# Head, seams and tail of a linear-attention-plus-MLP kernel: transposed weights from two queues, a root on another engine, work units placed anew

## The chip, the cores and the metric

The kernel runs on one core of a Trainium2 chip. The metric is the device time of one execution in microseconds (us). The core has five engines that work side by side, each through its own queue of instructions in order: PE (TensorE, matrix products; its weight loads are listed as PEld), DVE (VectorE), ACT (ScalarE), POOL (GpSimd) and SP (SyncE, which here only starts transfers). Transfers are started from the queues of SP and ACT and carried out by 16 DMA engines.

## The reference

Two branches share one input. `x` has 2048 rows of 512 numbers in bf16. Branch A is a linear attention of 32 heads of 16 with a learned feature map (softmax of a projection and of its negative); branch B is a two-layer network with the Mish activation and 1792 hidden units. Cut to what matters:

```python
xn = layernorm(x)                                   # eps 1e-5, no scale
q, k, v = heads(xn @ wqkv)                          # 32 heads of 16
pq, pk = q @ w_phi[h], k @ w_phi[h]
phi_q = concat(softmax(pq), softmax(-pq))           # 32 features
phi_k = concat(softmax(pk), softmax(-pk))
kv = sum_s phi_k[s]^T v[s];  z = sum_s phi_k[s]
o = (phi_q @ kv) / (phi_q @ z + 1e-6)
act = mish(xn @ w1 + b1)
out = x + o @ wo + act @ w2
```

## The kernel before

**Tiling.** The 2048 rows are 16 tiles of 128 rows, in four groups of four (`NT`, `NG`, `TPG`). The contraction over 512 is cut into four blocks of 128 (`KT`), the 1792 hidden units into 14 blocks (`FT`). The program is written in the order in which each engine issues it (a manual schedule), and a tile framework adds the waits between engines that the data and the buffers ask for. A queue never reorders: an instruction that waits holds up everything behind it on its engine.

**Weights.** `w_phi` is folded into the key and query weights. `load_turned` (L87) fetches 512 columns of `wqkv` transposed, with a DMA transpose, into `wT`; `fold` (L93) multiplies its four blocks with the block-diagonal `Wbd` (16 products of 128x128 in all) and evicts four results, to `wkp` for the keys at the start and to `wqp` for the queries in stage 2. In `fold` at the start ACT evicts three blocks and DVE one.

**Normalisation.** `ln_stats` (L110) takes the statistics of tiles on DVE and computes one over the root on POOL, as a power of -0.5 in two instructions; `ln_apply` (L125) writes the normalised tile `xn` on DVE. The first four tiles are then turned on PE (`ln_turn_pe`, four transposing products into PSUM and a copy into `xnT`), the others by DMA transposes of two tiles each (`ln_turn_dma`).

**Units of work on PE.** `project` (L149) makes 4 products of 128x128 by 128x512 into one PSUM buffer; `value` (L159) evicts it into `vext`, `logits` (L186) into `p_sb`. `hidden(n)` (L168) does the next n of the 56 first-layer units (4 groups times 14 blocks, group by group), each 4 products and one Mish on ACT into `acts`. `accumulate(g)` (32 small products into `pkv`) adds up keys times values for one group. `second_layer(t)` makes 14 products into `po`, `attend(h, i)` 8 small ones into `pnd`, whose four copies run on ACT, `project_out(h)` four for each of two tiles on top of `po`; `residual` adds x on DVE and stores. PSUM has five buffers for everything tagged `mm`, and one for `pkv` and `pnd`.

**Units of work on DVE and ACT.** `extremes(s)` subtracts maxima and minima of 16 on DVE; `exponentials(s)` is two instructions of 2048 on ACT; `normalise` sums and divides on DVE. For the queries `turn` then transposes the features by DMA into `qT`. `combine(h)` makes the denominators and weights on DVE for two tiles, adds the two halves and transposes the result by one DMA into `oT`.

**The order.** At the head: loads, constants, 12 warm-up products on an identity, statistics of tiles 0 to 3, `fold`, the four turns among the first logits, then `extremes(0)` with the normalisation of group 1 in its midst, four values, four hidden units. Then a loop over stages s = 0 to 3, written out as

```python
exponentials(s); accumulate(s - 1); value x2 (dve); logits(s + 1) x4 (act); value x2 (act)
ln_stats; normalise(s, 0) with ln_apply of group s + 2 inside; normalise(s, 1)
hidden((16, 14, 8, 10, 4)[s]); extremes(s + 1)
```

(stages 4 and 5 are the queries of groups 0 and 1). After it come `exponentials(4)`, `accumulate(3)`, `mask_kv`, `logits(5)`, `second_layer(0)`, `hidden(4)`, `extremes(5)`, `attend(0, 0)`, `second_layer(1)`, `attend(0, 1)`, `combine(0)`, `exponentials(5)`, and then a loop over eight pairs of tiles, h = 0 to 7, that interleaves `combine`, `project_out`, the logits of the last two query groups, `attend` for two pairs ahead and `second_layer` for two pairs ahead.

**The start of the queues.** SP: x tiles 0 and 1, `wT`, x tiles 4 to 7, `wv`, `w1`, x tiles 8 to 15. ACT: `wsrc` (w_phi), x tiles 2 and 3, `b1b`, then its first table load. Scalar activations need a table; each change between copies, Exp and Mish shows as a table load of 1.28 us.

Of the kernel before, what the change touches and what calls it, by code (L numbers as in the profile page):

```python
# [8 lines left out]
BF16 = mybir.dt.bfloat16  # L9
FP32 = mybir.dt.float32  # L10
# [7 lines left out]
def kernel(  # L18
# [12 lines left out]
    nc = tc.nc  # L31
# [52 lines left out]

    def load_turned(base_col):  # L87

        wT = lnp.tile([P, 4, 512], BF16, name="wT", tag="xn")
        nc.sync.dma_start_transpose(out=wT[:], in_=A_wqkv[:, base_col : base_col + D])  # L90
        return wT

    def fold(wT, dst, dve):  # L93

        for kt in range(KT):
            pf = ps.tile([P, 512], FP32, name="pfold", tag="mm")
            for j in range(4):
                nc.tensor.matmul(
                    pf[:, j * P : (j + 1) * P],
                    lhsT=wT[:, j, kt * P : (kt + 1) * P],  # L100
                    rhs=Wbd[:, j, :],
                    start=True,
                    stop=True,
                )
            if kt in dve:
                nc.vector.tensor_copy(dst[:, kt, :], pf[:])
            else:
                nc.scalar.copy(dst[:, kt, :], pf[:])
# [16 lines left out]
    def ln_apply(t0, n, mv, rstd, xn, at):  # L125
        for i in range(n):
            nc.vector.tensor_scalar(
                out=xn[:, at + i, :],
                in0=x_sb[:, t0 + i, :],
                scalar1=mv[:, i, 0:1],  # L130
                scalar2=rstd[:, i : i + 1],
                op0=ALU.subtract,
                op1=ALU.mult,
            )
# [172 lines left out]
            in1=KVmask[:, 128:136], op0=ALU.add, op1=ALU.mult,  # L307
        )

    nd_of, oT_of, po_of = {}, {}, {}  # L310

    def attend(h, i):

# [24 lines left out]
        )  # L338
        nc.scalar.copy(ds[:, i, :, :, 3, :], b.rearrange("p l (x h) -> p l x h", x=2))  # L339

    def combine(h):

        nm, ds = nd_of.pop(h)
        ds = ds[:].rearrange("p i l x j h -> p i l x (j h)")
        u = opool.tile([P, 2, 2, 32], FP32, name="u")
        w = opool.tile([P, 2, 32], FP32, name="w")
        f = opool.tile([P, 2, 2, 32, 2], BF16, name="f")
        ob = lnp.tile([P, 4, 512], BF16, name="ob", tag="xn")
        o_t = ob[:, 0:2, :]
        oT_of[h] = ob[:, 2:4, :].rearrange("p i (j c) -> p (i j) c", c=P)  # L350
        nc.vector.tensor_tensor(  # L351
            out=u[:], in0=ds[:, :, :, 0, :], in1=ds[:, :, ::-1, 1, :], op=ALU.mult
        )
        nc.vector.tensor_tensor(out=w[:], in0=u[:, :, 0, :], in1=u[:, :, 1, :], op=ALU.add)
        nc.vector.reciprocal(w[:], w[:])  # L355
        nc.vector.tensor_tensor(
            out=u[:], in0=ds[:, :, ::-1, 1, :],
            in1=w[:, :, None, :].to_broadcast([P, 2, 2, 32]), op=ALU.mult,
        )
        nc.vector.tensor_copy(  # L360
            f[:].rearrange("p i l c o -> p (i l c) o"),
            u[:].rearrange("p i l (c o) -> p (i l c) o", o=1).to_broadcast([P, 128, 2]),
        )
        v = nm.rearrange("p i l (c e o) -> p (i l c) e o", e=8, o=2)
        nc.vector.tensor_tensor(  # L365
            out=v, in0=v,
            in1=f[:].rearrange("p i l c o -> p (i l c) o")[:, :, None, :].to_broadcast([P, 128, 8, 2]),
            op=ALU.mult,
        )
        nc.vector.tensor_tensor(  # L370
            out=o_t, in0=nm[:, :, 0, :], in1=nm[:, :, 1, :], op=ALU.add
        )
        nc.sync.dma_start_transpose(out=oT_of[h], in_=o_t.rearrange("p i c -> p (i c)"))

    def second_layer(t):
        po = ps.tile([P, 512], FP32, name="po", tag="mm")
        po_of[t] = po
        for f in range(FT):
            nc.tensor.matmul(  # L379
                po[:], lhsT=acts[:, f, t * P : (t + 1) * P], rhs=w2_sb[:, f, :],  # L380
                start=(f == 0), stop=False,
            )

    def project_out(h):
        for i in range(2):
            po = po_of.pop(2 * h + i)
            for j in range(4):
                nc.tensor.matmul(  # L388
                    po[:], lhsT=oT_of[h][:, i * 4 + j, :], rhs=wo_sb[:, j, :],
                    start=False, stop=(j == 3),  # L390
                )
            residual(2 * h + i, po)

    def residual(t, po):
        y = x_sb[:, t, :]
        nc.vector.tensor_tensor(out=y, in0=po[:], in1=y, op=ALU.add)  # L396
        nc.sync.dma_start(o_v[:, t, :], y)


    nc.sync.dma_start(x_sb[:, 0:2, :], x_v[:, 0:2, :])  # L400
    with nc.allow_non_contiguous_dma(reason="tiny w_phi load"):
        nc.scalar.dma_start(wsrc[:], wphi_v)
    wT = load_turned(D)
    nc.scalar.dma_start(x_sb[:, 2:4, :], x_v[:, 2:4, :])
    nc.scalar.dma_start(b1b[:], b1_v[:, :])
    nc.sync.dma_start(x_sb[:, 4:8, :], x_v[:, 4:8, :])
    nc.sync.dma_start(wv[:], wqkv_v[:, :, 2 * D : 3 * D])
    nc.sync.dma_start(w1_sb[:], w1_v[:, :, :])
    nc.sync.dma_start(x_sb[:, 8:16, :], x_v[:, 8:16, :])

# [14 lines left out]
    nc.vector.tensor_copy(KVmask[:, 0:P], block[:].rearrange("p h d -> p (h d)"))  # L425
    nc.vector.tensor_copy(KVmask[:, P : P + 8], block[:, :, 0])
    nc.vector.tensor_copy(
        kvm[:].rearrange("p l j c -> p (l j) c")[:, :, 136:144],
        block[:, None, :, 0].to_broadcast([P, 8, 8]),
    )  # L430
# [2 lines left out]
    dve, act = nc.vector.tensor_copy, nc.scalar.copy  # L433

    warm = ps.tile([P, 4, P], FP32, name="warm", tag="mm")
    for _ in range(12):
        nc.tensor.matmul(
            warm[:], lhsT=ident[:], rhs=ident[:, None, :].to_broadcast([P, 4, P]),
            start=True, stop=True,
        )  # L440

    st0 = ln_stats(0, 2)
# [6 lines left out]
    st1 = ln_stats(2, 2)  # L449
    xn = lnp.tile([P, TPG, D], BF16, name="xn", tag="xn")  # L450
    ln_apply(0, 2, *st0, xn, 0)
    fold(wT, wkp, (3,))
    ln_turn_pe(0, xn, 0, dve)
    ln_turn_pe(1, xn, 1, act)
    pb = ps.tile([P, 512], BF16, name="pb", tag="mm")
    nc.tensor.transpose(pb[:, 0:FT], b1b[:], ident[0:FT, 0:FT])
    ln_apply(2, 2, *st1, xn, 2)
    logits(0, 0, act)
    for i in range(2, 4):
        ln_turn_pe(i, xn, i, dve)  # L460
    nc.vector.tensor_copy(b1f[:], pb[:, 0:FT])
    for i in range(1, TPG):
        logits(0, i, act)

    def normal(t0, st, xn):
# [6 lines left out]
    extremes(0, lambda: normal(TPG, st, xn))  # L472
    nc.sync.dma_start(w2_sb[:], w2_v[:, :, :])
    nc.sync.dma_start(wo_sb, wo_v[:, :, :])
    for i in range(TPG):
        value(i, act)
    hidden(4)

    for s in range(NG):
        exponentials(s)
        if s > 0:
            accumulate(s - 1)
        if s < NG:
            for i in range(2 if s else 0):
                value(s * TPG + i, dve)
        for i in range(TPG):
            logits(s + 1, i, act)
        if 0 < s < NG:  # L490
# [12 lines left out]
        if s == 2:
            fold(wT, wqp, ())
        hidden((16, 14, 8, 10, 4)[s])
        extremes(s + 1)


# [3 lines left out]
    for i in range(TPG):  # L512
        logits(5, i, act if i == 3 else dve)
    second_layer(0)
    hidden(4)
    extremes(5)
    attend(0, 0)
    second_layer(1)
    attend(0, 1)
    combine(0)  # L520
    exponentials(5)
    second_layer(2)
    attend(1, 0)
# [55 lines left out]
```

## Time and profile before

| | |
|---|---|
| median of 3 executions | 188.48 us |
| the profiled execution | 188.35 us |
| its span, first to last instruction | 186.6 us |
| PE busy | 176.2 us, 94% |
| DVE busy | 148.4 us, 80% |
| ACT busy | 127.0 us, 68% |
| POOL busy | 8.2 us, 4% |
| read from and written to memory | 6.84 MB, 2.10 MB |

The profile is of one execution. Its span is shorter than the execution's time because the time also holds what lies before the first and after the last instruction, 1.75 us together. Lines of the timeline give the start and the duration in us, the engine (SPq and ACTq are the queues that start transfers), the line of the kernel, the operation, the tile written and the tiles read, and in brackets how long the engine was idle before it and what ended that. "x4" merges four like instructions that follow one another. A busy PE says that products are under way, not that they run at full rate.

### The profile page before, as it was taken

How to read it: one execution, taken by the hardware profiler on the slowest of the kernel's cores; microseconds unless marked ns; L12 is line 12 of the kernel's file. 1: busy time of each engine (PE TensorE's matmuls, PEld its weight loads, DVE VectorE, ACT ScalarE, POOL GpSimd, SP SyncE). 2: the span in 40 equal slices, each digit the busy share in tenths (PEclk: the TensorE clock that was granted, in tenths of full speed). 3: DMA queues.
4: the chain of work that ended last, by engine and by line, in shares of the span. 5: the costliest groups of instructions: out<-in, count | busy, mean ns of one | idle time of the engine just before them, and what ended most of it. 6: DMA issues, size and time to landing. Idle time of an engine off the chain costs nothing.

```text
span 186.6 us, 2710 instructions
## 1 busy us (share of the span) xinstructions
PE 176.2 (94%) x1021; PEld 88.5 (47%) x1021; DVE 148.4 (80%) x255; ACT 127.0 (68%) x196; POOL 8.2 (4%) x22
## 2 busy tenths in 40 slices
PE   6699879999999999999999999799999999999982
PEld 2444334464444654644464555355554545455430
DVE  4989999978999899989997927299947696738742
ACT  2458999889887899969969859573842567244200
POOL 3403020000200000000000000000000000000000
PEclk9999999999999999999999999999999999999998
DMA  6996999000190000000002900973079303980732
GB/s 146 304 404 222 209 358 164 0 4 2 34 191 0 4 0 0 0 0 4 0 0 53 176 0 0 179 160 60 0 170 192 87 5 66 196 189 1 116 84 84
DMA packets 44217, 18.02 MB, mean 97 GB/s; under 512 B 36780, under 2 KB 43692, under 8 KB 44204
## 3 DMA queue, kind: packets, MB, share of 16 engines
q1 hardware_dynamic: 43376, 17.57, 40.1%
q10 hardware_dynamic: 828, 0.28, 0.6%
q8 instruction: 8, 0.13, 0.3%
q14 instruction: 5, 0.04, 0.1%
HBM read 6.84 MB, written 2.10 MB: 48 GB/s over the span
## 4 chain that ended last, share of the span: by engine, by line
PE 76%; DVE 9%; ACT 6%; DMA 5%; issue 1%; ACTq 0%; SPq 0%
PE ph L174 24%; PE pproj L154 20%; PE po L379 18%; PE po L388 6%; PE pkv L279 4%; PE pnd L323 4%; DMA ob<-ob 3%; ACT e L226 2%; DMA x_sb<-in_A_x_dram 2%; DVE stats L116 1%; DVE wv L365 1%; ACT acts L181 1%; DVE ob L370 1%; DVE w L355 1%; ACT wv L332 1%
## 5 line engine op out<-in xcount | busy, mean ns | idle before, releaser
L379 PE MATMUL po<-w_sb,acts 128*128 128x512 bf16 x224 | 50.8, 379 | 0.0
L174 PE MATMUL ph<-xnT,w_sb 128*128 128x512 bf16 x224 | 49.5, 379 | 1.2 <-ACT p_sb L192 1.2
L181 ACT ACTIVATE acts<-ph,b1f 128x512 bf16<-128x512 f32 x56 | 35.5, 694 | 3.8 <-PE ph L174 3.5
L174 PEld LDWEIGHTS <-w_sb 128*128 128x128 bf16 x224 | 21.9, 98 | 27.5 <-issue 1.4
L226 ACT ACTIVATE e<-e 128x2048 bf16<-128x2048 bf16 x16 | 29.7, 1902 | 7.0 <-DVE e L216 6.9
L379 PEld LDWEIGHTS <-acts 128*128 128x128 bf16 x224 | 21.4, 98 | 23.1
L154 PEld LDWEIGHTS <-xnT 128*128 128x128 bf16 x192 | 18.4, 98 | 22.9 <-DMA xnT<-xn 1.3
L192 ACT CAST p_sb<-pproj 128x512 bf16<-128x512 f32 x29 | 15.7, 586 | 9.7 <-PE pproj L154 9.7
L244 DVE TENSOR_REDUCE s<-e 128x128 f32<-128x2048 bf16 x8 | 18.2, 2279 | 1.6 <-ACT e L226 1.6
L396 DVE TENSOR_TENSOR x_sb<-po,x_sb 128x512 bf16<-128x512 f32 x16 | 10.6, 685 | 7.6 <-PE po L388 7.6
L388 PE MATMUL po<-wqk,ob 128*128 128x512 bf16 x64 | 15.1, 379 | 0.7 <-DMA ob<-ob 0.7
L154 PE MATMUL pproj<-wkp,xnT 128*128 128x512 bf16 x64 | 14.7, 379 | 0.8 <-DMA xnT<-xn 0.8
L154 PE MATMUL pproj<-wv,xnT 128*128 128x512 bf16 x64 | 15.1, 379 | 0.0
L332 ACT CAST wkp<-pnd 128x768 bf16<-128x768 f32 x8 | 6.4, 798 | 12.6 <-PE pnd L323 8.7
L154 PE MATMUL pproj<-wqk,xnT 128*128 128x512 bf16 x64 | 14.6, 379 | 0.2 <-DVE x_sb L396 0.2
L205 DVE TENSOR_TENSOR m<-p_sb 128x1024 bf16<-128x1024 bf16 x16 | 11.0, 686 | 3.9 <-ACT p_sb L192 3.9
L351 DVE TENSOR_TENSOR u<-ds 128x128 f32<-128x128 f32 x8 | 2.3, 289 | 12.8 <-ACT ds L339 12.8
L205 DVE TENSOR_TENSOR m<-m 128x512 bf16<-128x512 bf16 (+1 forms) x32 | 11.5, 358 | 1.1
L323 PE MATMUL pnd<-kvm,qT 128*128 128x144 bf16 x128 | 10.6, 226 | 1.1 <-ACT ds L339 1.1
L323 PEld LDWEIGHTS <-qT 128*128 128x128 bf16 x128 | 9.1, 98 | 5.0 <-issue 1.3
L116 DVE BATCH_NORM_STATS2 stats<-x_sb 128x6 f32<-128x512 bf16 x16 | 10.0, 680 | 1.2 <-DMA x_sb<-in_A_x_dram 1.2
L332 ACT CAST wv<-pnd 128x768 bf16<-128x768 f32 x8 | 6.3, 792 | 6.1 <-PE pnd L323 3.8
(64 smaller groups left out, 173.0 us busy)
## 6 DMA issues: line engine op xcount, KB each, us to landing
w_sb<-in_B_w_dram SPq DMA_DIRECT2D x2, 1792.0 KB, 8.7
out_dram<-x_sb SPq DMA_DIRECT2D x16, 128.0 KB, 1.9
x_sb<-in_A_x_dram SPq DMA_DIRECT2D x1, 1024.0 KB, 11.4
x_sb<-in_A_x_dram SPq DMA_DIRECT2D x1, 512.0 KB, 4.1
wv<-in_A_wqkv_dram SPq DMA_DIRECT2D x1, 512.0 KB, 5.0
wqk<-in_A_wo_dram SPq DMA_DIRECT2D x1, 512.0 KB
x_sb<-in_A_x_dram SPq DMA_DIRECT2D x1, 256.0 KB, 3.1
x_sb<-in_A_x_dram ACTq DMA_DIRECT2D x1, 256.0 KB, 3.5
```

What stands on the lines that cost most here:

```text
L116: nc.vector.bn_stats(stats[:, i, :], x_sb[:, t0 + i, :])
L154: nc.tensor.matmul(pp[:], lhsT=xnT[:, t, kt, :], rhs=w[:, kt, :], start=(kt == 0), stop=(kt == KT - 1),)
L174: nc.tensor.matmul(ph[:], lhsT=w1_sb[:, kt, f * P : (f + 1) * P], rhs=xnT[:, g * TPG : (g + 1) * TPG, kt, :], start=(kt == 0), stop=(kt == ...
L181: nc.scalar.activation(acts[:, f, g * 512 : (g + 1) * 512], ph[:], ACT.Mish, bias=b1f[:, f : f + 1])
L192: copy(p_of[s][:, i, :], pp[:])
L205: nc.vector.tensor_tensor(out=m[:], in0=src[:, :, 0:half], in1=src[:, :, half : 2 * half], op=op)
L226: nc.scalar.activation(v, v, ACT.Exp)
L244: nc.vector.reduce_sum(t[:], v.rearrange("p t l (c e) -> p (t l c) e", e=16), axis=AX.X)
L323: nc.tensor.matmul(blocks(pnd, pl, j, 144), lhsT=qT_of[h][:, i, pl * 4 + j, :], rhs=kvm[:, pl, j, :], start=True, stop=True,)
L332: nc.scalar.copy(to[:, :, 0:3, :], a)
L379: nc.tensor.matmul(po[:], lhsT=acts[:, f, t * P : (t + 1) * P], rhs=w2_sb[:, f, :], start=(f == 0), stop=False,)
L388: nc.tensor.matmul(po[:], lhsT=oT_of[h][:, i * 4 + j, :], rhs=wo_sb[:, j, :], start=False, stop=(j == 3),)
```

## The change

- `load_turned` can cut the transpose of `wT` by rows into halves from several queues; the first call uses SP and ACT. x tiles 2 and 3 and `b1b` move from ACT's queue to SP's, and `wv` goes ahead of x tiles 4 to 7.
- A first root (`root`, of the constant `eps`) is issued on ACT behind these transfers. For tiles 0 to 3 the roots are taken on ACT (`stats_head`), with a reciprocal on DVE (`apply_head`), for tile 0, tile 1, and tiles 2 and 3 together.
- Twelve warm-up products become eight; three small copies of constants move from DVE to POOL.
- The turn of tile 0 stands after the second block of `fold`; the logits of tiles 0 and 1 and the values of tile 0 come before the turns of tiles 2 and 3.
- Hidden units: 4 + (16, 14, 8, 10) + 4 become 5 + (19, 14, 8, 8) + 2. Two of the logits of group 1 are evicted by DVE.
- `attend(0, 1)` comes after 8 of the 14 products of `second_layer(1)`, and `extremes(5)` after it.
- `combine(3)` comes after `project_out(2)`; `combine(7)` is made in two halves, one for each tile; the last tile's output projection, residual and store are made in two column halves, stored from ACT's and SP's queues.

```diff
-    def load_turned(base_col):
+    def load_turned(base_col, queues=(nc.sync,)):
...
+        for i, queue in enumerate(queues):
+            queue.dma_start_transpose(
+                out=wT[:, :, i * n : (i + 1) * n],
+                in_=A_wqkv[i * n : (i + 1) * n, base_col : base_col + D],
+            )
...
-    wT = load_turned(D)
-    nc.scalar.dma_start(x_sb[:, 2:4, :], x_v[:, 2:4, :])
-    nc.scalar.dma_start(b1b[:], b1_v[:, :])
+    wT = load_turned(D, (nc.sync, nc.scalar))
+    nc.scalar.activation(root[:], eps[:], ACT.Sqrt)
+    nc.sync.dma_start(x_sb[:, 2:4, :], x_v[:, 2:4, :])
+    nc.sync.dma_start(wv[:], wqkv_v[:, :, 2 * D : 3 * D])
     nc.sync.dma_start(x_sb[:, 4:8, :], x_v[:, 4:8, :])
-    nc.sync.dma_start(wv[:], wqkv_v[:, :, 2 * D : 3 * D])
+    nc.sync.dma_start(b1b[:], b1_v[:, :])
...
-    for _ in range(12):
+    for _ in range(8):
...
+    def stats_head(t, n):
...
+        nc.scalar.activation(rstd[:], mv[:, :, 1], ACT.Sqrt, bias=eps[:])
+        return mv, rstd
+
+    def apply_head(t, n, mv, rstd):
+        nc.vector.reciprocal(rstd[:], rstd[:])
+        ln_apply(t, n, mv, rstd, xn, t)
+
+    st = stats_head(0, 1)
...
+    apply_head(0, 1, *st)
+    st = stats_head(1, 1)
+    fold(wT, wkp, (3,), {1: lambda: ln_turn_pe(0, xn, 0, act)})
+    apply_head(1, 1, *st)
+    ln_turn_pe(1, xn, 1, dve)
...
+    st = stats_head(2, 2)
+    for i in range(2):
+        logits(0, i, act)
+    nc.vector.tensor_copy(b1f[:], pb[:, 0:FT])
+    apply_head(2, 2, *st)
+    value(0, act)
+    ln_turn_pe(2, xn, 2, dve)
+    ln_turn_pe(3, xn, 3, act)
     for i in range(2, 4):
...
-    for i in range(TPG):
+    for i in range(1, TPG):
         value(i, act)
-    hidden(4)
+    hidden(5)
...
-            logits(s + 1, i, act)
+            logits(s + 1, i, dve if s == 0 and i < 2 else act)
...
-        hidden((16, 14, 8, 10, 4)[s])
+        hidden((19, 14, 8, 8)[s])
...
-    hidden(4)
+    hidden(2)
+    attend(0, 0)
+    second_layer(1, 0, 8)
+    attend(0, 1)
     extremes(5)
-    attend(0, 0)
-    second_layer(1)
-    attend(0, 1)
+    second_layer(1, 8)
...
-        if 0 < h < 7:
+        if h in (1, 3, 4, 5):
             combine(h + 1)
+        if h == 5:
+            combine(7, first)
+        if h == 6:
+            combine(7, last)
         project_out(h)
-        if h == 0:
-            combine(1)
+        if h in (0, 2):
+            combine(h + 1)
...
+            cuts = (slice(0, 256), slice(256, 512)) if (h, i) == (7, 1) else (slice(0, 512),)
+            for n, c in enumerate(cuts):
...
+                residual(2 * h + i, po, c, nc.sync if n or len(cuts) == 1 else nc.scalar)
```

More of the change, by code (lines that the diff above doesn't have):

```diff
@@ L77 @@
     ident = consts.tile([P, P], BF16, name="ident")
+    eps = consts.tile([P, 1], FP32, name="eps")
+    root = consts.tile([P, 1], FP32, name="root")
     mhalf = consts.tile([P, TPG], FP32, name="mhalf")
@@ L83, with fold @@
     ctx.enter_context(tc.manual_schedule())
-    def load_turned(base_col):
+    def load_turned(base_col, queues=(nc.sync,)):
         wT = lnp.tile([P, 4, 512], BF16, name="wT", tag="xn")
-        nc.sync.dma_start_transpose(out=wT[:], in_=A_wqkv[:, base_col : base_col + D])
+        n = D // len(queues)
+        for i, queue in enumerate(queues):
[3 more added lines that the diff above has]
+            )
         return wT
-    def fold(wT, dst, dve):
+    def fold(wT, dst, dve, behind={}):
         for kt in range(KT):
@@ L108, in fold @@
                 nc.scalar.copy(dst[:, kt, :], pf[:])
+            if kt in behind:
+                behind[kt]()
     def ln_stats(t0, n):
@@ L308, in mask_kv @@
         )
-    nd_of, oT_of, po_of = {}, {}, {}
+    nd_of, oT_of, po_of, tmp_of = {}, {}, {}, {}
     def attend(h, i):
@@ L339, in attend, with combine @@
         nc.scalar.copy(ds[:, i, :, :, 3, :], b.rearrange("p l (x h) -> p l x h", x=2))
-    def combine(h):
-        nm, ds = nd_of.pop(h)
+    def combine(h, parts=(slice(0, 2),)):
+        nm, ds = nd_of.pop(h) if parts[-1].stop == 2 else nd_of[h]
         ds = ds[:].rearrange("p i l x j h -> p i l x (j h)")
[L345 to L378, printed above, removed]
+        if h not in oT_of:
+            ob = lnp.tile([P, 4, 512], BF16, name="ob", tag="xn")
+            u = opool.tile([P, 2, 2, 32], FP32, name="u")
+            w = opool.tile([P, 2, 32], FP32, name="w")
+            f = opool.tile([P, 2, 2, 32, 2], BF16, name="f")
+            tmp_of[h] = ob[:, 0:2, :], u, w, f
+            oT_of[h] = ob[:, 2:4, :].rearrange("p i (j c) -> p (i j) c", c=P)
@@ new lines, in combine @@
+        o_t, u, w, f = tmp_of[h]
+        for q in parts:
+            n = q.stop - q.start
+            nc.vector.tensor_tensor(
+                out=u[:, q], in0=ds[:, q, :, 0, :], in1=ds[:, q, ::-1, 1, :], op=ALU.mult
+            )
+            nc.vector.tensor_tensor(
+                out=w[:, q], in0=u[:, q, 0, :], in1=u[:, q, 1, :], op=ALU.add
+            )
+            nc.vector.reciprocal(w[:, q], w[:, q])
+            nc.vector.tensor_tensor(
+                out=u[:, q], in0=ds[:, q, ::-1, 1, :],
+                in1=w[:, q, None, :].to_broadcast([P, n, 2, 32]), op=ALU.mult,
+            )
+            nc.vector.tensor_copy(
+                f[:, q].rearrange("p i l c o -> p (i l c) o"),
+                u[:, q].rearrange("p i l (c o) -> p (i l c) o", o=1).to_broadcast(
+                    [P, n * 64, 2]
+                ),
+            )
+            v = nm[:, q].rearrange("p i l (c e o) -> p (i l c) e o", e=8, o=2)
+            nc.vector.tensor_tensor(
+                out=v, in0=v,
+                in1=f[:, q].rearrange("p i l c o -> p (i l c) o")[:, :, None, :].to_broadcast(
+                    [P, n * 64, 8, 2]
+                ),
+                op=ALU.mult,
+            )
+            nc.vector.tensor_tensor(
+                out=o_t[:, q], in0=nm[:, q, 0, :], in1=nm[:, q, 1, :], op=ALU.add
+            )
+            nc.sync.dma_start_transpose(
+                out=oT_of[h][:, 4 * q.start : 4 * q.stop, :],
+                in_=o_t[:, q].rearrange("p i c -> p (i c)"),
+            )
@@ L379, in second_layer @@
+    def second_layer(t, f0=0, f1=FT):
+        if f0 == 0:
+            po_of[t] = ps.tile([P, 512], FP32, name="po", tag="mm")
+        po = po_of[t]
+        for f in range(f0, f1):
             nc.tensor.matmul(
                 po[:], lhsT=acts[:, f, t * P : (t + 1) * P], rhs=w2_sb[:, f, :],
-                start=(f == 0), stop=False,
+                start=(f == 0), stop=(t == NT - 1 and f == FT - 1),
             )
@@ L386, in project_out, with residual @@
             po = po_of.pop(2 * h + i)
[L387 to L397, printed above, removed]
+            cuts = (slice(0, 256), slice(256, 512)) if (h, i) == (7, 1) else (slice(0, 512),)
+            for n, c in enumerate(cuts):
+                for j in range(4):
+                    nc.tensor.matmul(
+                        po[:, c], lhsT=oT_of[h][:, i * 4 + j, :], rhs=wo_sb[:, j, c],
+                        start=False, stop=(j == 3 or len(cuts) == 2), skip_group_check=len(cuts) == 2,
+                    )
+                residual(2 * h + i, po, c, nc.sync if n or len(cuts) == 1 else nc.scalar)
+    def residual(t, po, c, queue):
+        y = x_sb[:, t, c]
+        nc.vector.tensor_tensor(out=y, in0=po[:, c], in1=y, op=ALU.add)
+        queue.dma_start(o_v[:, t, c], y)
+    nc.gpsimd.memset(eps[:], 1e-5)
     nc.sync.dma_start(x_sb[:, 0:2, :], x_v[:, 0:2, :])
@@ L424 @@
     nc.vector.memset(pkv[:, :, 0:432], 0.0)
-    nc.vector.tensor_copy(KVmask[:, 0:P], block[:].rearrange("p h d -> p (h d)"))
-    nc.vector.tensor_copy(KVmask[:, P : P + 8], block[:, :, 0])
-    nc.vector.tensor_copy(
+    nc.gpsimd.tensor_copy(KVmask[:, 0:P], block[:].rearrange("p h d -> p (h d)"))
+    nc.gpsimd.tensor_copy(KVmask[:, P : P + 8], block[:, :, 0])
+    nc.gpsimd.tensor_copy(
         kvm[:].rearrange("p l j c -> p (l j) c")[:, :, 136:144],
@@ L440 @@
         )
-    st0 = ln_stats(0, 2)
+    xn = lnp.tile([P, TPG, D], BF16, name="xn", tag="xn")
+    def stats_head(t, n):
+        stats = lnp.tile([P, n, nc.vector.BN_STATS_DIM], FP32, name="hstats", bufs=3)
+        mv = lnp.tile([P, n, nc.vector.BN_AGGR_DIM], FP32, name="hmv", bufs=3)
+        rstd = lnp.tile([P, n], FP32, name="hrstd", bufs=3)
+        for i in range(n):
+            nc.vector.bn_stats(stats[:, i, :], x_sb[:, t + i, :])
+        for i in range(n):
+            nc.vector.bn_aggr(mv[:, i, :], stats[:, i, :])
+        nc.scalar.activation(rstd[:], mv[:, :, 1], ACT.Sqrt, bias=eps[:])
[4 more added lines that the diff above has]
+    st = stats_head(0, 1)
     nc.vector.tensor_tensor(
@@ L448 @@
     )
[L449 to L454, printed above, removed]
+    apply_head(0, 1, *st)
[3 more added lines that the diff above has]
+    ln_turn_pe(1, xn, 1, dve)
     pb = ps.tile([P, 512], BF16, name="pb", tag="mm")
     nc.tensor.transpose(pb[:, 0:FT], b1b[:], ident[0:FT, 0:FT])
-    ln_apply(2, 2, *st1, xn, 2)
-    logits(0, 0, act)
+    st = stats_head(2, 2)
[6 more added lines that the diff above has]
+    ln_turn_pe(3, xn, 3, act)
     for i in range(2, 4):
-        ln_turn_pe(i, xn, i, dve)
-    nc.vector.tensor_copy(b1f[:], pb[:, 0:FT])
-    for i in range(1, TPG):
         logits(0, i, act)
@@ L525 @@
     attend(1, 1)
+    first, last = (slice(0, 1),), (slice(1, 2),)
     for h in range(2 * NG):
```

## The prediction

> **What bounds the kernel now.** I read the page's busy shares first, then the waits of TensorE, then the timeline of the first 30 us, then the landing times of the transposes, and last the chain of waits.
>
> ```profile
> PE 176.2 (94%) x1021; PEld 88.5 (47%) x1021; DVE 148.4 (80%) x255; ACT 127.0 (68%) x196; POOL 8.2 (4%) x22
> ```
>
> PE is the bound: all of the work besides the 4.23 us of warm-up products is needed after the change too. So the time can only move through PE's idle time: the head before the first logits, the gaps, and the tail. The waits of PE, longest first, are the list of what there is to win:
>
> ```profile
> PE ph L174 <- ACT p_sb L192: 1.2, 1, 1.2
> PE pfold L98 <- DMA wT<-in_A_wqkv_dram: 1.1, 1, 1.1
> PE pnd L323 <- ACT ds L339: 1.1, 1, 1.1
> PE pproj L154 <- DMA xnT<-xn: 0.8, 1, 0.8
> PE po L388 <- DMA ob<-ob: 0.7, 2, 0.6
> PE ptr L139 <- DVE wkp L106: 0.6, 1, 0.6
> PE pproj L154 <- DVE x_sb L396: 0.2, 1, 0.2
> ```
>
> (total, times, longest). The head, from the timeline (start, duration, engine, line):
>
> ```profile
> 1.30 3.34 SPq L90 DMA_TRANSPOSE wT<-in_A_wqkv_dram  x1
> 2.62 1.28 ACT L108 ACT_TABLE_LOAD   x1 [2.62 <-issue]
> 3.52 0.15 PEld L437 LDWEIGHTS <-ident 128*128 128x128 bf16 x1 [0.28 <-issue]
> 3.95 0.15 PEld L437 LDWEIGHTS <-ident 128*128 128x128 bf16 x1 [0.28 <-issue]
> 4.38 0.77 PEld L437 LDWEIGHTS <-ident 128*128 128x128 bf16 x4 [0.27 <-issue]
> 6.71 1.07 PE L98 MATMUL pfold<-Wbd,wT 128*128 128x128 bf16 x16 [1.06 <-DMA wT<-in_A_wqkv_dram]
> 8.98 1.04 PE L154 MATMUL pproj<-wkp,xnT 128*128 128x512 bf16 x4
> ```
>
> The transposed key weights land near 6.65, 5.35 after their issue; the first logits start at 8.98. Landing times of transposes, for xnT (256 KB each) and then for wT (512 KB):
>
> ```profile
> DMA to landing us min/median/max: 3.2/3.4/4.1
> ```
>
> ```profile
> DMA to landing us min/median/max: 4.4/4.9/5.4
> ```
>
> **Part 1, wT from two queues, and the root.** SP now issues one half of wT at 1.30 and ACT the other. Bounds for the second half: it goes out together with the first (about 1.3), or only after the first has landed. I take the second: the waits of this program are placed by the tile framework, and it orders transposes that come from different queues. No pair of queues transposes in the trace of before. The Trainium skill, "DMA: Bandwidth & Descriptors", section "Silent corruption: two transposing streams in flight at once", asks for just this wait, for the full completion of the earlier stream; by it the gain of a second queue is gone.
>
> First half: 256 KB, 3.4 (xnT's median) to 3.7 (5.35 less half of the 3.34 of issue), so it lands at 4.7 to 5.0; I take 5.0. Queued on ACT behind the waiting issue are the table load, the root of `eps`, both roots of the first tiles and all evictions of `fold`, and for these wait VectorE's normalised tiles and PE. Issue of the second half on ACT: 1.24 (the 256 KB transposes of ob and xnT) to 1.67 (half of 3.34), so ACT is free at 5.95 to 6.7; I take 6.6. Table load 1.28 gives 7.9. No row shows a root on ACT; the smallest ACT rows are 0.22 and 0.26 (the ds copies), I take 0.25 each (0.2 to 0.3): root 8.1, root of tile 0 at 8.4. Then VectorE: a reciprocal of one element per row (rows: 0.55 for 64, 0.94 for 128; by that slope 0.16), xn 0.38, bn_stats 0.68, aggregate 0.15 give 9.8; root of tile 1 at 10.1. Only then come ACT's four evictions of wkp 0, 1, xnT 0 and wkp 2 at 0.51 each: 12.2. **First logits at 12.3 instead of 8.98.**
>
> The second half's landing: issue 5.0 plus 3.4 (xnT's median) to 5.4 (wT's slowest), since x tiles 2 to 7, wv and w1 now go out from SP at about 3 to 6 and share the DMA engines; I take 4.4 (wT's quiet row), 9.4. The fold's 16 products of 0.056 end at 10.3, just covered by ACT until 10.1; if the transpose comes later, each us is a us of the end. If both halves left together, ACT would be free at 3.0, and the same chain gives first logits at 8.4.
>
> **Part 2, value tile and moved units.** From 12.3, PE does three products (0.86 each), waits 0.3 for tile 2's root and normalisation, two turns (0.4 each), another 0.3 for xnT, and then two logits, three values and five units, until 24.7. VectorE starts the statistics of tiles 4 to 7 after the copy of xnT 2 at 16.0: 2.66 for them, 2.98 for the first half of `extremes`, 0.68 for two xn, so the transpose is issued at 22.3 and lands at 25.7 (3.4). Logits of group 1 start there:
>
> ```profile
> 17.45 2.63 SPq L145 DMA_TRANSPOSE xnT<-xn  x2
> 20.77 3.63 PE L154 MATMUL pproj<-wkp,xnT 128*128 128x512 bf16 x16 [0.81 <-DMA xnT<-xn]
> 26.41 5.78 PE L174 MATMUL ph<-xnT,w_sb 128*128 128x512 bf16 x26 [1.15 <-ACT p_sb L192]
> ```
>
> 25.7 less 20.77 less the fifth unit (0.86) is **+4.1**; the wait on xnT is 1.0, not gone. The two logits of group 1 that VectorE now evicts (0.69 each) free two PSUM buffers while ACT is in the exponentials: the 1.15 at 26.41 goes, **-1.15**. What VectorE pays for it, 1.4, is covered by the unit count of stage 0 (4+16 becomes 5+19, 3.45 us of PE work). With no such cover PE would wait at `accumulate`; see rival 3.
>
> **Part 3, around the first products of `attend`.** The units ahead of `attend(0,0)` are 56 both times. But VectorE's `extremes(4)` and ACT's exponentials set when qT lands. In before it lands about 3.3 after 100.25, and `attend(0,0)` starts at 106.3, so 2.8 are spare; two units fewer in stage 3 and two fewer after `second_layer(0)` use 3.45 of it: a wait of 0.7. `attend(0,1)` now comes after 8 products (1.73) and waits 0.5 for the copies of the first (1.3 and a table load ahead of them). The old waits there, 1.06 on ds and 0.18 on ob, become 0 and 0.4. Together 1.6 against 1.24, about **+0.3**; between -1.2 (none of the new) and +1.0.
>
> **Part 4, the end.** `combine(3)` behind `project_out(2)`: the 0.20 at 142.89 goes, **-0.2**. The last `combine` in halves: 3.8 of VectorE for both becomes about 2.3 each, the fixed cost doubled. The first half runs while PE is in the second layer; it puts the second off to the residuals of tiles 10 and 11, which hold their PSUM buffers 2.2 longer, still ahead of `second_layer(15)`. The last transpose (128 KB, 2.4 to 3.1) then lands about when PE needs it: the 0.56 at 181.28 goes, **-0.56**.
>
> ```profile
> 178.18 3.05 DMA ob<-ob
> 181.23 0.05 issue
> 181.28 1.91 PE po L388 x8
> 183.19 0.02 issue
> 183.22 0.69 DVE x_sb L396
> ```
>
> Of the last residual of 0.69 only a half of about 0.4 stands behind the last product: **-0.3**. The second output queue hides nothing more: the output's 1.9 stays.
>
> **Part 5, eight warm-ups instead of twelve.** The weight loads above lie 0.43 apart up to 4.38 and then four fit into 0.77: PE runs at half rate for the first 3.0 us of work (the granted clock reads 1.00 there, so only the spacing tells it). Eight end near 4.8, so PE then idles until 9.4, 4.6 us, where it idled 1.06 and kept full rate. Bounds: nothing, if the rate is kept; or half rate again for some 3 us of work, of which PE's own waits in the head cover the rest: 1.2. I take 0.6, the middle, because 4.6 idle us lie between the one row (1.06, kept) and the start (cold). The skill's "TensorE: Matmul & The Clock Gate", section "Part 1: The HAM clock gate (the "warmup" mystery)", speaks against the edit: after an idle window of some 3.4 us the clock is halved; by it the whole 1.2 would be lost, and the sum be 0.6 higher.
>
> **Sum.** 4.1 - 1.15 + 0.3 - 0.2 - 0.56 - 0.3 + 0.6 = +2.79. The profiled execution took 188.35 (span 186.6 and 1.75 around it), 0.13 under the median of 188.48: 188.35 + 2.79 = 191.1. Everything else (KVmask copies on POOL, whose rows show it idle from 2.7 to 5.5; the loads on SP) costs nothing while POOL and SP are idle there; b1b and wv have 5 us to spare.
>
> **Rivals.** 1: *the two halves run together.* For it: nothing in the data makes one half need the other. Against: the wait above. First logits at 8.4, logits of group 1 at 21.6 (4.1 earlier), PE idle only briefly, so no half rate: 191.1 - 4.1 - 0.6 = 186.4, on the other side of 188.5. It decides if the second transpose's issue starts before 2. 2: *the second half lands late.* In 6.7 to 12 the DMA engines already move 349 to 410 GB/s; if the 1.28 MB of x and wv ahead are served first, at 0.38 MB per us, it lands 2.4 later, at 11.8, and PE, idle 7 us, restarts at half rate: 191.1 + 2.4 + 0.6 = 194.1. It decides from a landing of about 10.5. 3: *VectorE becomes the bound.* It is some 6 to 7 us later after group 1's logits, PE 6.4 later at `accumulate(0)` (2.95 and 3.45), but only 4.7 later at `accumulate(3)`, where before had 2.1 spare: 0.8 stay at a lag of 6, and at 7 or 8 PE waits about 1: 192.1. Against it: VectorE's own idle time, 1.46 at 42.3 among it, takes up lag.
>
> **How the numbers follow.** Forecast 0.47 (its own range 189.3 to 192.4), rival 1 0.13, rival 2 0.27, rival 3 0.13. Two per cent, about what a measurement of this kernel can tell from no change, is 3.8: below 184.7 and above 192.3. Faster by that needs rival 1 with 1.7 more than worked out: 0.07. Slower: nearly all of rival 2 and a part of rival 3 and of the forecast: 0.34. Within: 0.59. The range goes from 185.8, rival 1 with 0.6 more gained, to 194.6, rival 2 with 0.5 more lost.
>
> **What would show it.** Right: an ACT transpose issue that waits until about 5; the table load at 6 to 7; fold at 8.4 to 10.4; first logits near 12; no wait of ph on p_sb; a wait of pnd on qT; none on the last ob. Wrong: an ACT issue at once, first logits before 10, or a PE that idles in the second stage.

## The result, and the profile after

The changed kernel takes 194.25 us (193.50 to 195.02, 4 executions), the kernel before 188.48: a ratio of 1.0306, 95% interval 1.0252 to 1.0361. It is 5.8 us slower, where the forecast, 191.1, was 2.6 slower. (A fourth execution of before, 201.64, lies far from the other three, 188.34 to 188.62, and is left out.) The profiled execution took 193.95, with a span of 192.2 instead of 186.6.

From the page of the changed kernel, its first part and the row of TensorE's granted clock (40 slices of 4.8 us, in tenths; before, it reads 9 in all but the last):

```profile
PE 178.8 (93%) x1006; PEld 90.2 (47%) x1021; DVE 150.8 (78%) x264; ACT 127.4 (66%) x199; POOL 6.9 (4%) x22
...
PEclk9855999999999999999999999999999999999999
```

PE has as many products to make (four warm-ups fewer, four more of half the width at the end) and is busy 2.6 longer: it works slower in slices 3 and 4. The waits of PE (total, times, longest):

```profile
PE pfold L105 <- DMA wT<-in_A_wqkv_dram: 3.3, 1, 3.3
...
PE ptr L148 <- DVE xn L136: 1.3, 1, 1.3
PE pproj L163 <- ACT acts L190: 0.8, 1, 0.8
PE po L413 <- DVE x_sb L421: 0.7, 1, 0.7
PE pb L499 <- DMA b1b<-in_B_b_dram: 0.6, 1, 0.6
PE pnd L332 <- DMA qT<-e: 0.5, 1, 0.5
PE pnd L332 <- ACT ds L348: 0.4, 1, 0.4
```

The wait on `p_sb` (1.15) is gone and the last wait on `ob` with it, as the change meant. New are a wait for `wT` three times as long, one for tile 1's `xn`, one for `b1b`, and at the end one for VectorE's residual. The 0.8 ahead of group 1's logits, now put down to `acts`, stood at the same place before, put down to `xnT`. The head, from the timeline (start, duration, engine, line, in brackets the idle time before it):

```profile
1.29 1.32 ACTq L94 DMA_TRANSPOSE wT<-in_A_wqkv_dram  x1
...
2.65 1.28 ACT L430 ACT_TABLE_LOAD   x1 [2.65 <-issue]
...
4.90 1.33 SPq L94 DMA_TRANSPOSE wT<-in_A_wqkv_dram  x1
...
7.96 0.54 SPq L434 DMA_DIRECT2D b1b<-in_B_b_dram  x1
...
8.32 1.03 PE L105 MATMUL pfold<-Wbd,wT 128*128 128x128 bf16 x8 [3.30 <-DMA wT<-in_A_wqkv_dram]
...
11.94 0.61 PE L148 MATMUL ptr<-ident,xn 128*128 128x128 bf16 x4 [1.31 <-DVE xn L136]
...
13.18 0.19 PE L499 MATMUL pb<-ident,b1b 14*128 14x14 bf16 x1 [0.63 <-DMA b1b<-in_B_b_dram]
...
13.30 3.60 PE L163 MATMUL pproj<-wkp,xnT 128*128 128x512 bf16 x8
...
28.94 3.63 PE L163 MATMUL pproj<-wkp,xnT 128*128 128x512 bf16 x15 [0.77 <-ACT acts L190]
```

The half on ACT's queue goes at once and **SP's half waits for it**; SP's six other loads stand behind. The first logits start at 13.30 (8.98 before), and their eight products take 3.60, where four took 1.04. The stretch from 9 to 16 us (length, then busy time and instructions by engine, granted clock, DMA share, GB/s), first before, then changed:

```profile
9.00:16.00 7.00, 7.00 (x40) 3.45 (x40) 6.06 (x18) 4.40 (x8) 1.81 (x2) 1.00 1.05 390
```

```profile
9.00:16.00 7.00, 5.06 (x28) 2.85 (x26) 3.97 (x12) 2.90 (x6) 0.00 (x0) 0.50 1.05 383
```

Forty products against 28, at a clock of 1.00 against 0.50. In finer windows of the changed kernel the clock reads 1.00 up to 8.0, at the end of the wait for `wT` falls to 0.50 (8.0 to 8.5), and is back at 18.5, after 5 us of products without a pause. Past the head, how far the changed kernel lies behind, by the starts of like work less the work that was moved:

| start of | before | after | moved units | behind by |
|---|---|---|---|---|
| logits of group 1 | 20.77 | 28.94 | 0.86 | 7.3 |
| `accumulate(0)` | 39.37 | 49.01 | 3.45 | 6.2 |
| `project_out(0)` | 118.94 | 125.17 | 0 | 6.2 |
| `project_out(3)` | 152.52 | 158.39 | 0 | 5.9 |
| `project_out(7)` | 181.28 | 186.43 | 0 | 5.15 |
| span | 186.6 | 192.2 | 0 | 5.6 |

(186.43 is worked out: `project_out(6)` starts at 184.70, and its eight products take 0.216 each.) So the head loses 7.3, later edits win 2.15 back in three steps, and the end loses 0.45. The end, from the timeline: PE waits 0.68 between the two column halves.

```profile
188.57 0.60 PE L413 MATMUL po<-wqk,ob 128*128 128x256 bf16 x4 [0.68 <-DVE x_sb L421]
...
189.20 0.43 DVE L421 TENSOR_TENSOR x_sb<-po,x_sb 128x256 bf16<-128x256 f32 x1 [0.69 <-PE po L413]
```

### The profile page after: what moved, and what is told of

Same layout as the page of the kernel before. It is cut to its first block, busy times and chain, and to the rows that moved or that the text cites. A ratio compares the mean times of both kernels' runs of the same rounds, so it can differ in the third digit from the quotient of the medians.

```text
span 192.2 us, 2712 instructions
## 1 busy us (share of the span) xinstructions
PE 178.8 (93%) x1006; PEld 90.2 (47%) x1021; DVE 150.8 (78%) x264; ACT 127.4 (66%) x199; POOL 6.9 (4%) x22
## 4 chain that ended last, share of the span: by engine, by line
PE 50%; DVE 32%; DMA 6%; ACT 6%; issue 3%; SPq 1%; ACTq 0%
PE po L402 19%; PE pproj L163 11%; PE ph L183 9%; PE po L413 7%; DVE s L253 7%; DVE m L214 6%; DVE e L225 5%; DVE e L266 4%; PE pnd L332 3%; ACT e L235 3%; DVE r L261 3%; DMA b1b<-in_B_b_dram 3%; DMA wT<-in_A_wqkv_dram 2%; DMA ob<-ob 2%; ACT acts L190 2%
## 5 line engine op out<-in xcount | busy, mean ns | idle before, releaser
L163 PEld LDWEIGHTS <-xnT 128*128 128x128 bf16 x192 | 18.9, 101 | 24.5 <-issue 2.8
L201 ACT CAST p_sb<-pproj 128x512 bf16<-128x512 f32 x27 | 14.7, 585 | 10.2 <-PE pproj L163 10.2
L421 DVE TENSOR_TENSOR x_sb<-po,x_sb 128x512 bf16<-128x512 f32 (+1 forms) x17 | 10.7, 655 | 12.0 <-PE po L413 12.0
L163 PE MATMUL pproj<-wkp,xnT 128*128 128x512 bf16 x62 | 16.3, 412 | 1.2 <-ACT acts L190 0.8
L163 PE MATMUL pproj<-wv,xnT 128*128 128x512 bf16 x61 | 16.0, 396 | 0.2
L413 PE MATMUL po<-wqk,ob 128*128 128x512 bf16 (+1 forms) x67 | 15.1, 366 | 1.0 <-DVE x_sb L421 0.7
L413 PEld LDWEIGHTS <-ob 128*128 128x128 bf16 x68 | 6.5, 98 | 8.1 <-issue 0.9
L266 DVE TENSOR_TENSOR e<-e,r 128x2048 bf16<-128x2048 bf16 x8 | 9.8, 1226 | 0.3
```

The source lines that it names most:

```text
L163: nc.tensor.matmul(pp[:], lhsT=xnT[:, t, kt, :], rhs=w[:, kt, :], start=(kt == 0), stop=(kt == KT - 1),)
L201: copy(p_of[s][:, i, :], pp[:])
L266: nc.vector.tensor_tensor(out=vv, in0=vv, in1=r2[:, :, None, :].to_broadcast([P, 128, 8, 2]), op=ALU.mult)
L413: nc.tensor.matmul(po[:, c], lhsT=oT_of[h][:, i * 4 + j, :], rhs=wo_sb[:, j, c], start=False, stop=(j == 3 or len(cuts) == 2), skip_group_ ...
```

## The experiments

The theory after the result: the loss is (a) the wait of SP's half and what stands behind it, (b) TensorE's half rate, (c) the column halves; the other edits win what they were worked out to win. The rivals: the new order of the head costs by itself, or VectorE's extra work does. Times are medians; the kernel before ran beside them at 188.44 to 188.56.

**The edits behind the head.** The head of before with everything that the change does behind it, and the last tile whole:

```diff
 (head: loads, POOL's root, 12 warm-ups, order, value x4, hidden(4) as before)
-        hidden((19, 14, 8, 8)[s])
+        hidden((20, 14, 8, 8)[s])
-            cuts = (slice(0, 256), slice(256, 512)) if (h, i) == (7, 1) else (slice(0, 512),)
+            cuts = (slice(0, 512),)
```

> The head of before, whole (loads, POOL's root, 12 warm-ups, the order up to the first extremes, four values and four hidden units), with all that the change does behind it: logits of group 1 by VectorE, hidden (20, 14, 8, 8) and 2, the attend order, combine(3) and combine(7); the last tile whole. Theory A (all of the loss lies in the head and in the column halves): before's 188.4 less 1.15 (gap at 26.41), 0.36 (gap at 142.89) and 0.72 (last ob wait), plus 0.1 (attend waits): 186.3 (185.9 to 186.8). Rival (the gap at 26.41 or the last ob wait comes back elsewhere once the head is early, VectorE's 1.4 us more being paid at accumulate(0)): 187.4 to 188.4.

Measured: **186.53** (186.40 to 186.66), ratio 0.9894 (0.9882 to 0.9907). Theory A holds to 0.2. These edits are worth 2.0, and VectorE's 1.4 more do not come back as a wait. This is a version faster than both kernels.

**The column halves.** The last edit undone in the changed kernel:

```diff
-            cuts = (slice(0, 256), slice(256, 512)) if (h, i) == (7, 1) else (slice(0, 512),)
+            cuts = (slice(0, 512),)
```

> The changed kernel with the last tile's output projection, residual and store whole again; all else as changed. Theory A (the column halves cost time: TensorE's second half waits 0.68 for VectorE's read of the first half in the same PSUM buffer): that wait is gone, the last residual is 0.69 instead of about 0.4, and the time falls by 0.45, to 193.8 (193.5 to 194.0 as a median). Rival (as the prediction had it, the halves save 0.3): it rises by 0.3, to 194.5. No other wait changes.

Measured: 193.49 (193.05 to 193.68), ratio 1.0260 (1.0247 to 1.0273), at the lower edge of theory A's range. The halves cost 0.76 between the medians, 0.45 by the trace; the executions of the changed kernel spread by 1.5, so the size is uncertain, but the sign is not the one of the prediction. The wait on `x_sb` is gone.

**More warm-ups alone.** 24 in the changed kernel:

```diff
-    for _ in range(8):
+    for _ in range(24):
```

> The changed kernel with 24 warm-up products instead of 8, so that TensorE is busy from 1.4 to about 8.3 and the fold follows without a pause. Theory A (half rate after the idle time is the largest part of the loss): the weight loads of the first logits lie 0.22 apart instead of 0.43, and the time falls by 2.6 us, to about 191.6. Theory B (the late second half of wT alone; the rate costs nothing because TensorE waits for others in the head): within 0.5 us of 194.2. Theory C (the new order of the head, with roots on ScalarE, is what costs): within 0.5 us of 194.2.

Measured: 193.50 (192.96 to 194.68), ratio 1.0277 (1.0235 to 1.0318). Only 0.75 came back, less than the 1.5 by which the changed kernel's own executions spread; the 2.6 of theory A did not. The fold now runs at full rate (8.68, eight products in 0.61 instead of 1.03), but PE then waits for tile 1 and for `b1b`, and the half rate is back. From the timeline, and from the windows of this run:

```profile
13.91 0.10 PEld L499 LDWEIGHTS <-b1b 14*128 14x128 bf16 x1 [2.42 <-DMA b1b<-in_B_b_dram]
```

```profile
13.00:19.00 6.00, 4.87 (x12) 1.85 (x14) 1.51 (x7) 1.47 (x3) 0.00 (x0) 0.50 1.04 391
```

The clock fell at about 12.4, within this wait.

**`b1b`, 24 warm-ups, or both.** `b1b` on ACT's queue behind its half, the last tile whole, with two queues; first with 8 warm-ups, then with 24:

```diff
     wT = load_turned(D, (nc.sync, nc.scalar))
+    nc.scalar.dma_start(b1b[:], b1_v[:, :])
...
-    nc.sync.dma_start(b1b[:], b1_v[:, :])
```

> The changed kernel with b1b on ACT's queue behind its half of wT and the last tile whole; wT still from two queues, 8 warm-up products. It completes the two-by-two of warm-ups (8 or 24) and b1b's place (SP behind the loads, or ACT) with two queues: e4_whole_tail 193.49 (neither), e12 189.49 (both), and 24 warm-ups alone gave 0.75. Theory A (either one alone leaves TensorE at half rate, since both idle times are long enough): the wait of 0.6 to 1.0 for b1b goes, the half rate of 9 to 18 is only a little shorter; 192.2 (191.6 to 192.9). Rival (b1b's wait is what brings the half rate): 189.5 to 190.5.

> The changed kernel, wT still from two queues, with 24 warm-up products, b1b on ACT's queue behind its half of wT, and the last tile whole. Of the loss in the head it leaves only the wait of SP's half (landing at 8.3) and the new order. Theory A (the rate is the largest single loss, and with 24 warm-ups it came back only because TensorE waited 2.3 for b1b): ACT's half still goes first, TensorE keeps full rate from 5.7 on, first logits near 11.3, time 189.8 (189.3 to 190.6). Rival 1 (the half rate returns in any case with the sparse work of the head): 191.8 to 192.8. Rival 2 (b1b on ACT turns the order of the halves as it did ahead of the half): ACT's half lands late, about 200.

Measured: with 8 warm-ups 192.42 (191.45 to 193.14), ratio 1.0193 (1.0173 to 1.0212); with 24, **189.49** (189.38 to 190.09), ratio 1.0056 (1.0042 to 1.0070). Theory A both times. From 193.49, `b1b` alone wins 1.1 and both together 4.0, where warm-ups alone had won 0.75 (from 194.25): in these kernels TensorE's rate is kept only if neither gap is left, the one before the fold and the one for `b1b`. With both closed the rate holds, even through the 1.31 that PE still waits for tile 1, and the first logits start at 11.51, eight products in 1.90:

```profile
8.48 0.61 PE L105 MATMUL pfold<-Wbd,wT 128*128 128x128 bf16 x8
...
11.51 1.90 PE L163 MATMUL pproj<-wkp,xnT 128*128 128x512 bf16 x8
```

**The wait itself.** The two queues put into the kernel before, and nothing else:

```diff
-    wT = load_turned(D)
+    wT = load_turned(D, (nc.sync, nc.scalar))
```

> The kernel before with only the transpose of wT cut into halves from SP and ScalarE; 12 warm-ups, all loads and the whole order as before. One half waits for the other and the second lands near 8.3 instead of 6.65, so TensorE idles 2.7 us instead of 1.06. Theory A: 1.6 us more, about 190.1, if 2.7 us of idle time leave the full rate, and about 192 if they do not. Theory B: 1.6 us more in both cases. Theory C (not the transpose, but the new order of the head costs): within 0.5 of 188.5. That two queues help after all: 187 or less.

Measured: 191.60 (191.32 to 192.61), ratio 1.0177 (1.0149 to 1.0206). Theory A, with the rate not kept (about 192). Here too ACT's half goes at 1.30 and SP's waits until 4.92 and lands at 8.33 instead of 6.65: 1.7 later. The rest of the 3.2, about 1.5, is put down to the rate: clock 0.50 from about 10 to 13, after a wait of 1.64 (not the 2.7 expected), where before waited 1.06 and kept it. Timeline, then one of the windows:

```profile
4.92 1.31 SPq L92 DMA_TRANSPOSE wT<-in_A_wqkv_dram  x1
...
8.33 1.07 PE L103 MATMUL pfold<-Wbd,wT 128*128 128x128 bf16 x16 [1.64 <-DMA wT<-in_A_wqkv_dram]
```

```profile
11.00:12.00 1.00, 1.00 (x3) 0.30 (x2) 0.10 (x1) 0.39 (x1) 0.00 (x0) 0.50 1.11 331
```

**One queue.** The changed kernel with `load_turned(D)`:

> The changed kernel with wT transposed by one transfer from SP, all else as changed, the order of the loads too. wT should land near 6.7 and TensorE idle 1.7 us before the fold. Theory A (late second half, and half rate after the long idle time): both go, about 189.4. Theory B (late half alone): 1.6 us less, about 192.6. Theory C (the new order of the head): at most 0.5 us less, about 193.7.

Measured: 191.06 (190.23 to 192.29), ratio 1.0160 (1.0125 to 1.0196): 3.2 faster than with two, between theories A and B. `wT` lands near 5.85, but PE, after 8 warm-ups, still loads weights 0.43 apart until 13.8: the wait went, the half rate stayed. With `b1b` on ACT's queue, 12 warm-ups and the last tile whole as well:

```diff
-    wT = load_turned(D, (nc.sync, nc.scalar))
+    nc.scalar.dma_start(b1b[:], b1_v[:, :])
+    wT = load_turned(D)
...
-    for _ in range(8):
+    for _ in range(12):
```

> The changed kernel with wT whole from SP alone, b1b on ACT's queue behind wsrc, 12 warm-up products, and the last tile whole. Theory A (what was lost is the wait between two transposes and the half rate, not the new order of the head): wT lands at about 5.9, TensorE is at full rate from then on, first logits near 9, and with the gains behind the head 187.3 (186.8 to 188.3). Rival B (the new order of the head costs by itself, with its waits for the normalised tiles and its sparse work, so that half rate lasts to about 13 as it did with one queue and 8 warm-ups, 191.06): 191.06 less 0.45 and 0.2, 190.4.

Measured: **187.23** (186.85 to 187.60), ratio 0.9930 (0.9917 to 0.9942), as theory A has it. The timeline of this run: the fold's products run at full rate, with no wait.

```profile
5.83 0.62 PE L105 MATMUL pfold<-Wbd,wT 128*128 128x128 bf16 x8
...
8.86 1.90 PE L163 MATMUL pproj<-wkp,xnT 128*128 128x512 bf16 x8
```

Then each of the two alone: 12 warm-ups with `b1b` on SP, and `b1b` on ACT with 8 warm-ups.

> The changed kernel with wT whole from SP, 12 warm-up products and the last tile whole; b1b stays on SP behind x tiles 4 to 7. With the next kernel it splits what e5_one_b1b_warm12_whole won over e2_one_queue (191.06 to 187.23) into the four warm-up products and b1b's place. Theory A (the rate of TensorE: 12 warm-ups reach up to wT's landing at 5.8, so that fold and all behind it run at full rate): 187.5 (187.2 to 188.2). Rival (b1b's late arrival is what cost, and keeps TensorE waiting ahead of the first logits): 189.5 to 190.3.

> The changed kernel with wT whole from SP, b1b on ACT's queue behind wsrc, 8 warm-up products, and the last tile whole. Theory A (the rate): TensorE idles some 0.9 ahead of fold and runs at half rate to 13 or 14 as it did with one queue and b1b on SP; 189.8 (189.0 to 190.4). Rival (b1b's place): 187.2 to 188.0.

Measured: 190.37 (188.80 to 191.60), ratio 1.0069 (1.0043 to 1.0095), and 189.27 (186.89 to 190.44), ratio 1.0000 (0.9970 to 1.0031). For the first theory A was wrong by 2.9 and the rival holds: `b1b` on SP makes PE wait 1.4, and in eight of twelve executions the mean clock falls to 0.98 or 0.99. The other four, 188.80 to 188.83 at a clock of at least 0.998, suggest a price of the wait without that fall, 1.6 over 187.23. For the second theory A holds for the median, but the kernel varies from one execution to the next: three of twelve at 186.9 to 187.4, the others at 188.5 to 190.4, from one program.

**Fewer warm-ups before.** The kernel before with 4 instead of 12:

> The kernel before with 4 warm-up products instead of 12 and nothing else changed; its weights still land at 6.65. It measures the idle time of TensorE by itself, without any later transfer. Theory A (a TensorE that is idle for 2 to 3 us ahead of its work runs it at half rate for some 4 us more): weight loads 0.43 apart until about 10.5 to 11, fold in 2.1 instead of 1.07, time 188.4 plus 1.5 to 2.5, 189.9 to 190.9. Rival B (the rate is not a matter of the warm-ups): 188.4, within 0.3.

Measured: 189.71 (189.10 to 189.94), ratio 1.0059 (1.0042 to 1.0076): 1.2 more, a little below theory A's 1.5 to 2.5, and not rival B's nothing. In its timeline the sixteen products of the fold take 1.89; before, 1.07:

```profile
6.83 1.89 PE L98 MATMUL pfold<-Wbd,wT 128*128 128x128 bf16 x16 [3.53 <-DMA wT<-in_A_wqkv_dram]
```

**The other order of the halves.** `b1b` on ACT's queue ahead of ACT's half, in the changed kernel:

> The changed kernel with the load of b1b on ScalarE's queue ahead of its half of the transpose, as it stood on that queue before. In the changed kernel the transpose of b1b (line pb) waits for this load until 13.18 and the first logits stand behind it. Theory A and B: the first logits start at about 12.6 instead of 13.3, 0.7 to 0.9 us less, about 193.4. Theory C (the roots' chain sets the first logits): within 0.3 of 194.2.

Measured: **200.28** (199.77 to 201.43), ratio 1.0636 (1.0602 to 1.0671), against an expected small gain. The halves changed places: SP's goes at 1.31 and ACT's waits for it, as the prediction had assumed. But SP's loads no longer wait, and ACT's half lands behind them. Timeline, then DMA issues (operation, times, median us to landing):

```profile
5.18 1.75 ACTq L94 DMA_TRANSPOSE wT<-in_A_wqkv_dram  x1
...
17.56 1.03 PE L105 MATMUL pfold<-Wbd,wT 128*128 128x128 bf16 x8 [7.59 <-DMA wT<-in_A_wqkv_dram]
```

```profile
wT<-in_A_wqkv_dram ACTq DMA_TRANSPOSE x1, 12.3
```

To tell whether these loads are the cause, the same kernel with `wv`, x tiles 4 to 7, `w1` and x tiles 8 to 15 issued from ACT's queue behind its half:

> The kernel of e3_b1b_act (SP's half of wT first, ACT's half issued at 5.2 and landed only at 17.55), with wv, x tiles 4 to 7, w1 and x tiles 8 to 15 issued from ACT behind its half instead of from SP. Theory A (the late half is served with the bulk loads that SP had issued ahead of it in time): with no bulk load ahead it lands 3.4 to 4.4 after its issue, at 8.6 to 9.6; the roots of the head now stand behind four more issues on ACT (some 2 us), so first logits near 14 and a time of 194 to 196.5. Rival (a transpose from ACT's queue is slow by itself, or slow because the other queue transposed just before): it lands more than 9 us after its issue, as before, and the time stays at 199 to 201.

Measured: 193.26 (192.79 to 193.68), ratio 1.0246 (1.0229 to 1.0264), 0.7 below theory A's range, and the landing as theory A has it:

```profile
wT<-in_A_wqkv_dram ACTq DMA_TRANSPOSE x1, 3.4
```

The Trainium skill, "DMA: Bandwidth & Descriptors", section "Issuing engines are not separate DMA queues", says that transfers from all queues end on the same 16 engines and interleave. The 12.3 against 3.4 agrees, and shows how much bulk loads ahead, from the other queue, can cost a small transfer.

**The new order of the head.** The 187.23 kernel lies 0.70 behind the one with the old head. In it, as in the changed kernel, PE waits 1.3 for tile 1, whose normalisation stands on VectorE behind `fold`'s fourth copy:

```diff
+    apply_head(1, 1, *st)
     fold(wT, wkp, (3,), {1: lambda: ln_turn_pe(0, xn, 0, act)})
-    apply_head(1, 1, *st)
```

> The kernel of e5_one_b1b_warm12_whole with apply_head of tile 1 issued ahead of fold instead of behind it, so that on VectorE tile 1 is normalised ahead of fold's fourth copy. Theory A (ScalarE, with two roots, three evictions of fold and one turn ahead, sets the first logits): TensorE's wait of 1.3 for tile 1 goes, but the first logits then wait for ScalarE's last eviction, 8.6 instead of 8.86, and tiles 2 and 3 are normalised about 0.9 earlier, which takes TensorE's later wait of some 0.6: 187.23 less 0.5, 186.7 (186.3 to 187.1). Rival (the wait for tile 1 is the whole loss): 187.23 less 1.3, 185.9, faster than the kernel with the old head. Rival 2 (the loss lies behind the head, in ScalarE's evictions ahead of group 1's logits): 187.2, no change.

Measured: **186.59** (186.14 to 186.71), ratio 0.9889 (0.9870 to 0.9909): theory A. The 1.3 goes, 0.33 of it turns into a wait for ACT's copy of `xnT`, and the new order is level with the old.

## Why the prediction was wrong

The step that failed is the cost of the head: parts 1 and 2 gave it +4.1 and part 5 another 0.6, and it cost 7.0. The wait between the halves was put on the wrong queue, the wait for `b1b` was put at nothing, and the clock term of 0.6, with a bound of 1.2, was worth 2.9.

The measured path from before to after, each step the difference of two medians:

| step | us |
|---|---|
| before to old head with the later edits (188.50 to 186.53) | -2.0 |
| to the new order and ACT's roots, one queue, rate kept (187.23) | +0.7 |
| to two queues, rate kept (189.49) | +2.3 |
| to `b1b` on SP and 8 warm-ups (193.49) | +4.0 |
| to column halves (194.25) | +0.8 |

The kernel of the third step has 24 warm-ups, since PE must be kept busy until 8.3, and `b1b` behind ACT's half. The 4.0 of the fourth step is 1.1 for `b1b`'s place and then 2.9 for the warm-ups; taken the other way round, warm-ups first, the shares are others (0.75 first), since each gap brings the half rate back. The forecast had +4.1 and +0.6 for the head, -1.61 for the edits behind it and -0.3 for the halves; the runs have +7.0, -2.0 and +0.8.

- **Part 1, the wait: right that there is one, wrong on its side.** The prediction let "the second half goes out ... only after the first has landed" mean that ACT waits, and held up ACT's table load and roots. SP waited. ACT was early (table load at 2.65, not 6.6), the half landed at 8.3, not 9.4, and yet the first logits came at 13.3, not 12.3. The chain that was costed did not exist; the one that did (SP's loads, tile 1 behind the copy on VectorE, `b1b`) was not costed. That 12.3 came within 1.0 of the start is luck. Its own sign of being wrong, an ACT issue at once, was there. Which half goes first hung on the order of the loads: moving one 3.5 KB load turned it round.
- **"b1b and wv have 5 us to spare": wrong for `b1b`.** Issued at 7.96 behind three loads, it was awaited until 13.18, 5.2 later. Its place cost 1.1 with 8 warm-ups, and it brings the half rate back where more warm-ups had lifted it.
- **Part 5, the clock: sign right, size wrong.** The term was 0.6, bounded by 1.2. In the kernel before, 4 warm-ups instead of 12 did cost that bound, 1.2 (189.71). In the new head, with `b1b` early, 24 warm-ups instead of 8 are worth 2.9 (192.42 to 189.49). The bound took the half rate to last some 3 us of work, as at the start; in the changed kernel the loads of weights of its first logits and values lie 0.43 apart until 18.0, behind a head of short bursts and waits. The Trainium skill, "TensorE: Matmul & The Clock Gate", section "Part 1: The HAM clock gate (the "warmup" mystery)", has a free-running window of some 3.4 us, and a point of change that varies between runs. The spread from 186.89 to 190.44 of one kernel is in keeping with it, though only one of its executions was profiled, and in the changed kernel the clock fell after 3.3 of waiting. But in the run with 24 warm-ups the rate fell at 12.4, only 2.5 after the fold's last product and with 0.40 of work between, so less than the page's idle window was enough there.
- **Part 2, `p_sb`: right.** -1.15 forecast; the lag falls from 7.3 to 6.2.
- **Part 3: nearly right.** Waits of 0.5, 0.4 and 0.2 were measured where 0.7, 0.5 and 0.4 were forecast, 1.1 against the old 1.24: -0.1 instead of +0.3. (Copies on ACT need no table load of their own: in before they follow Exp at 25.80 and Mish at 107.09 without one. Only the first use and changes between Exp and Mish show one.)
- **Part 4: -0.2 and -0.56 right, -0.3 wrong.** Measured -0.36 and -0.72, by the steps of the lag from 6.23 to 5.87 and 5.15. Of the column halves the term left out that the second half's products must wait until VectorE has read the first out of the same PSUM tile; 0.45 to 0.76 instead of -0.3.
- **Rivals.** 1 (both halves at once) did not occur; running them without the wait was not tried. 2 (the second half lands late) did not happen either, since the half landed at 8.3; that its 194.1 lies next to the measured 194.25 is luck. Late landing is what the run at 200.28 shows, at 17.55. 3 (VectorE the bound) is refuted: from `accumulate(0)` to `accumulate(3)` PE takes 53.39, and before 55.11 less two moved units of 0.86, 53.38.

## What to carry to other kernels

When a wait joins two queues, cost it from both sides, and list for each side all that stands behind, down to the smallest load and its first reader. Treat TensorE's rate as something that the whole head must hold: look at the spacing of weight loads as well as at the clock, and close the long gaps up to the first dense stretch, all of them, since closing one of two won 0.75 or 1.1 and closing both won 4.0. Run a part of a change by itself: here the edits behind the head were worth 2.0, and a head that cost 7.3 hid them.

## What the runs showed of the hardware

- A 256 KB transpose from ACT's queue took 12.3 us to land when SP had issued 4.0 MB of loads before it, and 3.4 when all but the first 0.25 MB of them came behind it.
- The granted clock reads 1.00 while the rate at the start is still half: in the one-queue run with 8 warm-ups the weight loads lie 0.43 apart until 13.8 at a mean clock of 0.998. 0.50 was read only later, after a wait: from 8.3 on in the changed kernel, from 12.4 in the one with 24 warm-ups.
- One program, with 8 warm-ups, spread from 186.89 to 190.44, while the kernel before, whose 12 warm-ups end 1.06 ahead of the fold, stayed within 188.38 to 189.04 in the same comparison.
- The 512 KB transpose of `wT` took 2.40 to 2.58 us to issue and about 4.5 to land in the five one-queue runs with x tiles 2 and 3 behind it on SP, and 3.34 to 3.43 and about 5.4 in the three with them beside it on ACT's queue.
